# Second heads' root one exp later, part of a k norm on GpSimd, and first reciprocals behind the third heads' puts, in the opening of a fused attention and MoE kernel

## The chip, the cores and the metric

The kernel runs on one core of a Trainium2 chip. The metric is the device time of one execution in microseconds (us); lower is better. The core has five engines that run side by side, each through its own queue in order: TensorE (PE: matmuls and transposes), VectorE (DVE), ScalarE (ACT: exp, gelu, Ln, and some copies), GpSimd (POOL: elementwise work between SBUF tensors, and the issue of some DMAs) and SyncE (SP: the issue of most DMAs). Engines wait for one another through semaphores. Matmul results land in PSUM; everything else is in SBUF.

## The reference

Eight batches, 12 heads, 448 positions, head size 64. Queries and keys are RMS-normed with a gain, attention is a plain softmax, and its output goes through a two-layer MLP with a tanh-gelu:

```python
def rmsnorm(x, g):
    rms = np.sqrt(np.mean(x * x, axis=-1, keepdims=True) + 1e-06)
    return x / rms * g
q_n, k_n = (rmsnorm(q, g_q), rmsnorm(k, g_k))
scores = (1.0 / np.sqrt(64)) * np.matmul(q_n, k_n.transpose(0, 1, 3, 2))
scores = scores - np.max(scores, axis=-1, keepdims=True)
attn = np.exp(scores)
attn = attn / (np.sum(attn, axis=-1, keepdims=True) + 1e-09)
x = np.matmul(attn, v)            # then [B, S, H * D] as x of 3584 x 768
h = x @ w_in                      # 768 x 2048
g = 0.5 * h * (1.0 + np.tanh(c * (h + 0.044715 * h * h * h)))
return g @ w_out                  # 2048 x 768
```

Inputs and output are float32; the kernel computes its matmuls in bfloat16.

## The kernel before

The work goes batch by batch: attention of batch b + 1 is woven into the second MLP matmul of batch b. Nothing is scheduled by a planner: every engine does its instructions in the order in which the Python code issues them, and the code places them by hand. Only the attention of batch 0, which has no MLP work beside it, is touched by the change. It is made by `first_attention`.

The 12 heads of a batch are three groups of four, c = 0, 1, 2 ("first heads", "second heads", "third heads"). A group has seven tiles of 64 keys, t = 0 to 6. One `unit(0, c, t)` is four score matmuls (`sc`, two PSUM buffers) and one exp of 128 x 896 on ScalarE. So there are 21 units, numbered 0 to 20; unit 7 is the first of the second heads, unit 14 the first of the third heads. `first_attention` takes two plans: `side` (functions done ahead of a numbered unit) and `mid` (functions done behind a numbered unit). An entry `(8, f, g)` in `mid` issues f and g behind unit 8, each to its own engine's queue.

What a group needs before its first unit, for q and for k:

- `loads` brings the raw tiles, `square` squares them (ScalarE for the first heads, GpSimd after), `total` sums the squares on DVE;
- `rsqrt` makes the inverse root on ScalarE, as a Ln and an Exp with scale -0.5. `near` names the tensors (0 for q, 1 for k) whose root is written to PSUM, into `roots`, for DVE to read; the others' root goes to SBUF, into `rinvs`, for GpSimd, which reads SBUF here;
- `normed` multiplies raw by root on DVE or GpSimd (`nrmq`, `nrmk`); `turn` transposes on TensorE into the PSUM tiles `tp`; `put` copies the transposed q to `qT` and the transposed k times the gain column `gcol` to `kT`, on DVE. `t_first` is key tiles 0 to 3, `t_rest` is 4 to 6.

The gain column and the bound `shift`, which the exps subtract, come from the small tile `grow` with g_q and g_k in it: two DMAs (line 83), then products on GpSimd (`gprod`, `gbf`, lines 626 and 627), then GpSimd's first `normed` for the first heads' q.

What a group leaves: `products(0, c, 0)` sums the exps over keys by matmuls with ones, `turned` transposes these sums to `st` on DVE (line 358), `recips` takes the reciprocal and transposes back to `rb` (lines 364, 365), `products(0, c, 1)` is exps times v, and `quad_x` multiplies that by `rb` into `xT` (line 378). Both kinds of products of the first and of the second heads are written to the same two PSUM banks, `oall`: each has to wait until DVE has read the one before. The sums of the third heads go to two other banks (`spared`).

GpSimd's queue in this part holds, in order: the products of `grow`, a part of the first heads' q norm, the squares of the second heads, the issue of v's load, the squares of the third heads, six DMA issues of the first MLP weight (`w_in_part`, `win`, line 604), the norm of the third heads' q, two more of these issues, squares of batch 1, and issues of the second weight and the next v.

When the last exp of batch 0 is done, the last products follow, and the first MLP matmuls (`mm1_pair`, tile `hh`) start.

## Time and profile before

| what | value |
|---|---|
| time, median of 3 runs | 412.72 us (412.53 to 412.81) |
| the profiled execution, its own time | 412.78 us |
| its span (first to last instruction) | 410.9 us |
| TensorE busy | 399.3 us (97%) |
| ScalarE, DVE, POOL busy | 274.0, 256.0, 124.4 us |
| granted TensorE clock | 1.0 throughout |
| first exp, last exp of batch 0 starts | 9.93, 29.75 us |
| first MLP matmul starts | 32.86 us |

From 8 to 31 us, the time in which the first attention runs, DVE is busy 21.0, ScalarE 21.8 and POOL 22.6 of the 23 us.

In the lines of the profile, times are microseconds from the span's start. A line of the timeline has the start, the length, the engine, the source line, the operation, the tiles it writes and reads (out<-in, without buffer numbers), their shape, and how many instructions are merged into it; square brackets hold the idle time of the engine before it and what ended that. Instructions of one engine overlap a little: the next one starts some 0.05 to 0.1 us before the end of the one before. A line of the chain of waits has the start, the length and the work that the end of the program was waiting for at that time.

### The profile page before, as it was taken

How to read it: one execution, taken by the hardware profiler on the slowest of the kernel's cores; microseconds unless marked ns; L12 is line 12 of the kernel's file. 1: busy time of each engine (PE TensorE's matmuls, PEld its weight loads, DVE VectorE, ACT ScalarE, POOL GpSimd, SP SyncE). 2: the span in 40 equal slices, each digit the busy share in tenths (PEclk: the TensorE clock that was granted, in tenths of full speed). 3: DMA queues.
4: the chain of work that ended last, by engine and by line, in shares of the span. 5: the costliest groups of instructions: out<-in, count | busy, mean ns of one | idle time of the engine just before them, and what ended most of it. 6: DMA issues, size and time to landing. Idle time of an engine off the chain costs nothing.

```text
span 410.9 us, 8083 instructions
## 1 busy us (share of the span) xinstructions
PE 399.3 (97%) x3337; PEld 209.1 (51%) x3337; DVE 256.0 (62%) x414; ACT 274.0 (67%) x367; POOL 124.4 (30%) x102
## 2 busy tenths in 40 slices
PE   8889998999999999999999999999999999999996
PEld 3354554455555555555555555555555555555564
DVE  4999638845689357963688466982698604990010
ACT  5995387737975689738877579648878249744301
POOL 5991306492103540082302740063400900000000
PEclk9999999999999999999999999999999999999999
DMA  8999997869712947229922848309822511111033
GB/s 280 233 237 216 201 195 243 194 143 299 138 48 62 249 62 190 67 62 257 191 54 64 201 114 196 77 19 243 145 54 66 116 33 38 41 40 40 0 77 78
DMA packets 65572, 54.06 MB, mean 132 GB/s; under 512 B 37376, under 2 KB 60544, under 8 KB 65536
## 3 DMA queue, kind: packets, MB, share of 16 engines
q1 hardware_dynamic: 53184, 41.48, 39.1%
q0 software_dynamic: 12128, 11.80, 18.4%
q8 instruction: 26, 0.43, 0.4%
q10 hardware_dynamic: 224, 0.28, 0.2%
q14 instruction: 10, 0.08, 0.1%
HBM read 45.61 MB, written 11.01 MB: 138 GB/s over the span
## 4 chain that ended last, share of the span: by engine, by line
PE 88%; ACT 4%; DVE 4%; DMA 1%; POOL 1%; issue 0%; SPq 0%; DVEq 0%; ACTq 0%
PE o L408 35%; PE h L387 23%; PE t L298 8%; PE t L442 8%; PE t L349 8%; PE hh L442 4%; ACT ex L302 4%; DVE ss L156 2%; DMA rawq<-in_q_dram 1%; POOL g L151 1%; PE o L349 1%; DVE st L358 1%; PE tp L256 1%; DVE rb L365 1%; ACT g L447 0%; PE sc L298 0%
## 5 line engine op out<-in xcount | busy, mean ns | idle before, releaser
L408 PE MATMUL o<-wout,g 128*128 128x384 bf16 (+1 forms) x912 | 156.8, 324 | 0.0
L302 ACT ACTIVATE ex<-t,shift 128x896 bf16<-128x896 f32 x147 | 137.5, 1005 | 26.2 <-PE t L298 24.8
L408 PEld LDWEIGHTS <-g 128*128 128x128 bf16 x912 | 83.6, 98 | 68.0 <-issue 19.0
L387 PE MATMUL h<-xT,win 128*128 128x448 bf16 x504 | 96.5, 353 | 0.0
L156 DVE TENSOR_REDUCE ss<-sq 128x14 f32<-128x896 f32 (+3 forms) x43 | 44.3, 1037 | 53.6 <-ACT sq L149 50.7
L387 PEld LDWEIGHTS <-win 128*128 128x128 bf16 x504 | 49.3, 98 | 46.0
L393 ACT ACTIVATE g<-h 128x448 bf16<-128x448 f32 x84 | 45.6, 543 | 28.2 <-PE h L387 23.1
L422 DVE COPY osb<-o 128x384 f32<-128x384 f32 x51 | 27.7, 544 | 53.3 <-PE o L408 52.2
L298 PE MATMUL t<-qT,kT 64*64 64x448 bf16 x588 | 40.2, 360 | 1.7 <-DVE xT L373 1.1
L447 ACT ACTIVATE g<-t 128x896 bf16<-128x896 f32 x14 | 12.1, 914 | 43.5 <-PE t L442 43.5
L617 POOL COPY mark<-es 1x1 bf16<-1x1 bf16 x6 | 1.1, 176 | 129.8 <-DVE es L320 129.8
L442 PEld LDWEIGHTS <-win 128*128 128x128 bf16 x264 | 25.7, 98 | 24.8 <-issue 2.1
L238 POOL TENSOR_TENSOR nrmq<-rawq,rinv 128x896 bf16<-128x896 f32 (+1 forms) x21 | 34.8, 1659 | 10.1 <-DVE o L223 9.7
L442 PE MATMUL t<-xT,win 128*128 128x448 bf16 x168 | 33.5, 352 | 0.0
L151 POOL TENSOR_TENSOR sq<-rawq 128x896 f32<-128x896 f32 x9 | 15.1, 1681 | 57.3 <-DMA rawq<-in_q_dram 33.5
L298 PEld LDWEIGHTS <-kT 64*64 64x64 bf16 x672 | 16.5, 105 | 30.5 <-issue 24.3
L238 POOL TENSOR_TENSOR nrmk<-rawk,rinv 128x896 bf16<-128x896 f32 x19 | 31.9, 1679 | 0.0
L349 PE MATMUL t<-ex,vb 64*64 64x448 bf16 x588 | 31.6, 350 | 0.0
L365 DVE STREAM_TRANSPOSE rb<-rc 128x896 f32<-128x896 f32 x24 | 26.7, 1112 | 0.8
L349 PEld LDWEIGHTS <-vb 64*64 64x64 bf16 x672 | 19.6, 107 | 12.7 <-issue 2.9
L358 DVE STREAM_TRANSPOSE st<-t 128x448 f32<-128x448 f32 x42 | 24.6, 625 | 2.1 <-ACT ex L302 1.9
L323 DVE TENSOR_TENSOR e<-ex 128x896 bf16<-128x896 bf16 x32 | 19.4, 607 | 8.8 <-ACT ex L302 8.5
(89 smaller groups left out, 334.9 us busy)
## 6 DMA issues: line engine op xcount, KB each, us to landing
out_dram<-osb SPq DMA_DIRECT2D x54, 192.0 KB, 2.7
rawq<-in_q_dram SPq DMA_DIRECT2D x23, 448.0 KB, 4.6
rawk<-in_k_dram SPq DMA_DIRECT2D x23, 448.0 KB, 5.1
vb<-in_v_dram POOLq DMA_DIRECT2D x8, 672.0 KB, 6.7
win<-in_moe_w_in_dram POOLq DMA_DIRECT2D x8, 384.0 KB, 15.2
wout<-in_moe_w_out_dram POOLq DMA_DIRECT2D x2, 1536.0 KB, 26.4
qT<-nrmq SPq DMA_TRANSPOSE x19, 5.0
kT<-nrmk SPq DMA_TRANSPOSE x19, 4.4
```

Source lines behind the costliest of these rows:

```text
L156: nc.vector.reduce_sum(sss[b][:, c, "qk".index(n), hs, ts], sqs[n, b, c][:, hs, ts], axis=AX.X)
L238: eng.tensor_mul(nrms[n, b, c][:, ts].rearrange("p t a d -> p a t d"), raws[n, b, c][:, :, ts], root[:, :, ts].to_broadcast([P, 2, m, D]),)
L298: nc.tensor.matmul(sc[r * R:(r + 1) * R, a, :S], kT[rs, c, t, r], qT[b][rs, c, :, r], start=True, stop=True,)
L302: nc.scalar.activation(ex[:, t], sc[:, :, :S], AF.Exp, scale=scale, bias=shift)
L349: nc.tensor.matmul(o[r][a * D:(a + 1) * D], vb[b % 2][rs, 2 * c + a, i] if what else ones[rs], es[i][rs, a], start=(i == 0), stop=(i == n ...
L358: nc.vector.transpose(st[:, r].rearrange("p a b -> p (a b)"), oas[0][r])
L365: nc.vector.transpose(rb.rearrange("p r s -> p (r s)"), rc.to_broadcast([128, 2 * S // 32, 32]))
L387: nc.tensor.matmul(h[:, :S], win[:, c, f * 128:(f + 1) * 128], xT[b][:, c], start=(c == 0), stop=(c == HP - 1),)
L393: nc.scalar.activation(g[:, f, (b % 2) * S:(b % 2 + 1) * S], h[:, :S], AF.Gelu_apprx_tanh)
L408: nc.tensor.matmul(o, g[:, f, i * 128:(i + 1) * 128], wout[:, f, lo:hi], start=(f == 0), stop=(f == nf - 1),)
L422: nc.vector.tensor_copy(osb[:, lo:hi], o)
L442: nc.tensor.matmul(h[:, j, :S], win[:, c, f * 128:(f + 1) * 128], xT[b][:, c], start=(c == 0), stop=(c == HP - 1),)
```

## The change

Four things in the opening, all in the code for batch 0:

1. g_k is loaded by ScalarE's DMA queue, behind its half of the first q; it was loaded by GpSimd's queue behind g_q.
2. The root of the second heads is made behind the fourth exp (unit 3) instead of the third (unit 2). Before it, the rest of the first heads' k is normed, turned and put: the norm ahead of both sums, the turn and put behind unit 1. The put of the rest of the second heads' k moves behind the sums of the third heads' squares.
3. Of the second heads' k, `t_rest` is normed by GpSimd instead of DVE. For that, `rsqrt` writes the k root of the second heads to SBUF also (the new argument `also`, one more small Exp). GpSimd's new norm comes behind the square of the third heads' q; the square of the third heads' k and the six issues of `win` come behind it.
4. The first `recips` (reciprocal and transpose for the first heads) move on DVE from behind `turned` in slot 8 to slot 12, behind the puts of the third heads' q and first k tiles, and directly ahead of the first `quad_x`.

```diff
-    for i, row in enumerate((g_q, g_k)):
-        nc.gpsimd.dma_start(
+    def load_g(i, row, eng):
+        eng.dma_start(
             grow[:, i].rearrange("(j p) d -> j p d", j=2)[:, 0],
             row.rearrange("(j d) -> j d", j=2),
         )
+    load_g(0, g_q, nc.gpsimd)
...
-    def rsqrt(b, c=slice(0, NCH), ns=both, near=(), ts=slice(0, NT), twice=False):
+    def rsqrt(b, c=slice(0, NCH), ns=both, near=(), ts=slice(0, NT), twice=False, also=()):
...
         to_sbuf([n for n in range(2)[ns] if n not in near])
+        to_sbuf(also)
...
     for go in halves:
         go()
+    load_g(1, g_k, nc.scalar)
     nc.scalar.preload_act_table_set(EXP_SET)
...
     square(0, 2, "q", nc.gpsimd)
-    square(0, 2, "k", nc.gpsimd)
-    w_in_part(0, 2)
-    w_in_part(1, 2, range(1))
...
+    normed(0, 0, "k", nc.vector, t_rest)
     total(0, 1, "q")
-    normed(0, 0, "k", nc.vector, t_rest)
-    total(0, 1, "k")
...
-           (1, lambda: idle(2, warm())),
-           (2, lambda: rsqrt(0, 1, near=(0, 1)), lambda: idle(2, warm())),
-           (3, lambda: turn(0, 0, "k", t_rest), lambda: put(0, 0, "k", t_rest),
+           (1, lambda: turn(0, 0, "k", t_rest), lambda: put(0, 0, "k", t_rest),
+            lambda: total(0, 1, "k"), lambda: idle(2, warm())),
+           (2, lambda: idle(2, warm())),
+           (3, lambda: rsqrt(0, 1, near=(0, 1), also=(1,)),
             lambda: normed(0, 1, "q", nc.vector), lambda: normed(0, 1, "k", nc.vector, t_first),
-            lambda: normed(0, 1, "k", nc.vector, t_rest), lambda: idle(2, warm())),
+            lambda: normed(0, 1, "k", nc.gpsimd, t_rest), lambda: square(0, 2, "k", nc.gpsimd),
+            lambda: w_in_part(0, 2), lambda: w_in_part(1, 2, range(1)),
+            lambda: idle(2, warm())),
...
-           (6, lambda: turn(0, 1, "k"), lambda: put(0, 1, "k", t_first),
-            lambda: put(0, 1, "k", t_rest)),
+           (6, lambda: turn(0, 1, "k"), lambda: put(0, 1, "k", t_first)),
            (7, lambda: total(0, 2, "q"), lambda: total(0, 2, "k"),
-            lambda: products(0, 0, 0, 0, 3)),
-           (8, lambda: products(0, 0, 0, 3), lambda: turned(), lambda: recips(),
+            lambda: put(0, 1, "k", t_rest), lambda: products(0, 0, 0, 0, 3)),
+           (8, lambda: products(0, 0, 0, 3), lambda: turned(),
             lambda: rsqrt(0, 2, near=(1,)), lambda: normed(0, 2, "q", nc.gpsimd),
...
            (12, lambda: turn(0, 2, "q"), lambda: put(0, 2, "q"), lambda: turn(0, 2, "k"),
-            lambda: put(0, 2, "k", t_first), lambda: quad_x(0, 0),
+            lambda: put(0, 2, "k", t_first), lambda: recips(), lambda: quad_x(0, 0),
             lambda: put(0, 2, "k", t_rest)),
```

## The prediction

> **What bounds the kernel now.** I read the page first. Its share list of the chain that ended last gives TensorE nearly all of it:

> ```profile
> PE 88%; ACT 4%; DVE 4%; DMA 1%; POOL 1%; issue 0%; SPq 0%; DVEq 0%; ACTq 0%
> ```

> From 32.9 us on TensorE works almost without a hole, so whatever the change does before that point reaches the end at its full size, and a gain that is eaten before 32.9 is worth nothing. All edits lie before it. Second view: the chain of waits, 8 to 34 us (start, us, what). It is the time in which the first batch's attention runs.

> ```profile
> 2.20 6.04 DMA rawq<-in_q_dram
> ...
> 8.30 3.33 POOL g L151 x2
> ...
> 23.51 7.30 ACT ex L302 x8
> 30.81 0.04 issue
> 30.86 0.38 PE os L349 x4
> 31.24 1.69 PE o L349 x28
> ```

> The 21 exps of ScalarE (pitch 0.89 us) set the pace, but at three places they are held: the second heads' root (12.78), the second heads' first scores (17.09), the third heads' transposes (23.51, idle 0.29 before it). And POOL's work hangs on the landing of the second heads' q at 8.23, which no edit moves. Third view: the timeline of POOL (start, us, operation).

> ```profile
> 12.50 1.69 POOL L151 TENSOR_TENSOR g<-rawq 128x896 f32<-128x896 f32 x1
> 14.14 1.68 POOL L151 TENSOR_TENSOR sq<-rawk 128x896 f32<-128x896 f32 x1
> 15.76 3.79 POOL L604 DMA_DIRECT2D win<-in_moe_w_in_dram  x6
> 19.70 1.68 POOL L238 TENSOR_TENSOR nrmq<-rawq,rinv 128x896 bf16<-128x896 f32 x1
> ```

> POOL runs without a hole from 8.30, and the third heads' normed q (19.70 to 21.38) is at its end. Fourth: DVE, and TensorE beside it.

> ```profile
> 20.03 0.33 DVE L364 RECIPROCAL rc<-st 128x28 f32<-128x28 f32 x1
> 20.39 1.11 DVE L365 STREAM_TRANSPOSE rb<-rc 128x896 f32<-128x896 f32 x1
> 21.43 1.11 DVE L238 TENSOR_TENSOR nrmk<-rawk,root 128x512 bf16<-128x512 f32 x2
> 22.60 0.62 DVE L269 COPY qT<-tp 128x896 bf16<-128x896 bf16 x1
> 23.18 0.48 DVE L265 TENSOR_SCALAR kT<-tp,gcols 128x512 bf16<-128x512 bf16 x1
> 23.59 1.14 DVE L378 TENSOR_TENSOR xT<-o,rb 128x448 bf16<-128x448 f32 x2
> ```
> ```profile
> 22.00 0.56 PE L256 MATMUL tp<-ident,nrmq 128*128 128x128 bf16 x7
> 24.57 0.38 PE L298 MATMUL sc<-qT,kT 64*64 64x448 bf16 x4 [0.46 <-ACT ex L302]
> 24.76 0.78 PE L349 MATMUL o<-ex,ones 64*64 64x448 bf16 x12
> 25.47 0.38 PE L298 MATMUL sc<-qT,kT 64*64 64x448 bf16 x4
> ```

> To be seen: the second sum products (24.76) begin 0.03 us after quad_x frees the bank `oall` (23.59 + 1.14 = 24.73). They stand in front of the scores at 25.47, which the exp at 26.20 needs. That wait is closed already; its slack is small. The products end 0.57 us after 24.76, at 25.33, and scores lead their exp by 0.44 us (23.08 to 23.51), so scores at 25.76 would still serve 26.20: slack 0.43 us.

> **Part 1, g_k by ScalarE's queue.** By the rows of `grow`, g_q is issued at 1.30 and lands 3.7 us later at 4.97; g_k at 2.04, landing 4.0 later at 6.02; gprod starts 0.15 after that. ScalarE's own issue at 0.75 took 0.42 and landed after 3.35 us; so a g_k issued at 1.20 lands near 4.6, and gprod starts behind g_q at 5.1. ScalarE's table load moves from 1.20 to about 1.65 and ends at 2.9; the first square waits for q until 3.89, which hides the 0.42. One landing more among eight rotating semaphores makes SP's load of the third k wait for the first q half (3.87 instead of issue at 3.74): nothing, as that k lands at 11.8 and is squared at 14.9. POOL's normed q then waits for the root (6.23) instead of g, runs 6.3 to 7.34 instead of 7.02 to 8.06, and the first exp moves by 0.72, from 9.93 to 9.21.

> **Part 2, root behind the fourth exp.** Four exps from 9.21 end their pitch at 12.84; the k sums are done at 12.74 as before, since POOL's squares hang on the landing. The root comes at 12.84 instead of 12.78; Ln, root and the added rinv take 0.57 (the same three at 18.94 to 19.52). Exp 4 starts at 13.41, 0.73 earlier. But normed q, its transposes and puts follow the root: 13.39 start, q done 14.50, transposes 14.56, next scores 15.06, k transposes to 15.93, kT put 15.97 to 16.45, scores 16.51, exp 7 at 16.94 (17.09 before). Exps 6 and 7 wait 0.28 and 0.56 us, and **0.15 of the 0.73 is left.** POOL's 384-wide part is not in the trace: between 1.04 (512 wide) and nothing; by the slope to 1.68 (896 wide) it is 0.83 us, 14.14 to 14.97, before TensorE needs it at 15.4. I take that, as 384 is nearest to the 512 row; it stands in POOL's chain below, so at nothing the whole sum would be 0.79 less, at 1.04 it would be 0.21 more.

> **Part 3, what POOL's order now does.** From 14.14: normed k part (pitch 0.79), square of third k (1.62), six win issues (3.80), all ahead of normed q. It starts at 20.35 instead of 19.70 and ends at 22.03 instead of 21.38. The two last win issues, two squares, wout, v follow 0.65 later; win is first read at 32.86, with no wait on it shown, and that read moves back too, by more. Landing costs nothing then.

> **Part 4, reciprocals behind the puts.** DVE's normed k is now ready at 20.9 (was 22.54), but the put of q stands next and needs POOL's q: transposes 22.09 (22.03 + 0.06), done 22.65; put q 22.69; put k 23.27 to 23.75. So DVE idles 1.8 us, and the reciprocals, which ran 20.03 to 21.50 before, come after it: reciprocal 23.67, transpose 24.03 to 25.15, then quad_x with 0.10 delay (33.96 to 34.06 at the last such pair) and 1.15 for both halves: 25.25 to 26.40 instead of 24.73. Exps before this are at 23.44 and on, 0.07 early. TensorE's products get the second half-bank at 26.43; three groups at 0.19 remain, or two, so the scores come at 26.81 to 27.00 and exp 16 at 27.25 to 27.43 instead of 26.20. **The wait passed to quad_x costs 1.67, the slack takes 0.43, and exp 16 is 1.05 to 1.24 late.**

> **The end of the stage.** From these scores, DVE's second st transpose follows as now (25.47 to 26.64, 1.17): 28.09 instead of 26.64. From there to the end of the second quad_x DVE has no hole (26.64 to 31.36, 4.72), so 32.81; TensorE's last products overwrite `oall` and wait for it, and the first matmul of the MoE, 32.86 before (31.36 + 1.50), comes at 34.31. The exps end at 32.0 and do not bound it. Sum: **+1.45 us**, +1.34 to +1.53 by the two ends above, +1.27 if the 0.10 is also 0.03 as between the other dependent DVE rows, and by the ends for POOL's part +0.66 to +1.66. TensorE's rows behind are the same instructions in the same order.

> A question of its own is whether POOL's issues keep their length. The six took 0.63 to 0.69 us each (15.76 to 19.56) while DVE was busy 3.92 of the 4 us from 16 to 20, with copies and tensor_scalars from PSUM among its rows; so the sum uses 3.80 for the six. [...]

> **Rivals.**
> 1. *Not slower: POOL's q comes in time.* If normed q ends by 20.3, put and reciprocals run early enough that exp 16 is not held; the exps keep 0.15 plus the 0.29 wait and a little, and the kernel ends 0.3 to 0.7 us faster (412.0 to 412.4). Against: that needs POOL 1.7 us ahead of rows that follow each other without a hole from a landing at 8.23. The whole start gain, 0.73, is the most that could be kept, and it stays inside 0.2%. Chance 0.05.
> 2. *The late quad_x is partly covered.* Were the slack before exp 16 larger (TensorE's ends are modelled) and DVE's next rows tighter, 0.3 to 0.8 would be left: 413.0 to 413.5. For it: the idle 0.59 us of DVE before 26.64. Against: those products are late themselves. Chance 0.12.
> 3. *A second wait joins.* [...] So 1.45 plus 0.3 to 2.0: 414.5 to 416.2. [...] Chance 0.10. [...]
> 4. *The forecast,* 413.7 to 414.8. Chance 0.73.

> **The numbers.** The profiled execution took 412.78 (span 410.9 and 1.88 around it); the median of the three runs is 412.72, lowest 412.53. 412.78 + 1.45 = 414.23, and less the 0.06 between profile and median 414.2. The range takes all of the forecast, the upper half of rival 2 and the lower part of rival 3: 413.3 to 415.0. A difference of about 0.2% (0.83 us) is what a measurement can tell. Faster by more needs over 0.83 us, more than the whole start gain: 0.03. Within: the rest of rival 1 and most of rival 2, 0.13. Slower: 0.84.

> **What would show it.** In the changed profile: first exp near 9.2; exp 7 near 16.9; POOL's third normed q from 20.3 to 22.0; DVE idle before the qT copy near 22.7, released by TensorE's transposes; reciprocal near 23.7 instead of 20.0; the second sum products split, waiting on DVE's xT to 26.4; an exp idle of over 1 us near 26 to 27; the first `hh` matmul near 34.3. It is wrong if POOL's q ends before 21.4, or if quad_x ends after 26 and the exps still run on without a hole, or if the first `hh` matmul is at 33.5 or before.

## The result, and the profile after

The changed kernel takes 415.61 us (median of 8 runs, 413.86 to 417.52), the kernel before 412.76 beside it (8 runs, 412.30 to 413.58): ratio 1.007, 95% interval 1.0048 to 1.0093. It is slower, as forecast, but by 2.85 us instead of 1.45. The runs differ in the granted clock of TensorE, and that is part of the answer: the three with a mean clock of 0.998 or more took 413.86, 414.72 and 415.53 us, the five below it 415.37 to 417.52. So runs are counted below by whether their mean clock was under 0.998 ("low clock").

The profiled execution is the longest of the eight, 417.52 us (span 415.7), so it shows the costs at their largest. Its first `hh` matmul starts at 37.70 instead of 32.86, 4.84 later; from there to the end of the span it is 378.0 us in both, so the whole loss lies ahead of `hh`. The chain of waits of the changed kernel, 8 to 40 us (start, us, what), against the one shown of before, which held neither v nor `rb`:

```profile
8.45 3.26 POOL g L154 x2
11.71 10.79 DMA vb<-in_v_dram
...
22.54 0.76 PE o L353 x12
...
26.26 1.12 DVE rb L369
27.38 0.02 issue
27.41 0.64 DVE xT L382
28.04 0.04 issue
28.08 1.86 PE o L353 x12
```

Two things are on the chain. The reciprocals (`rb`) and `quad_x` (`xT`) stand there as the prediction had them. But the load of v stands ahead of them: it was issued at 11.71, about as before (11.56), and while the first of its sixteen parts landed at 17.7, the last did at 22.50 (18.5 before). The timeline of ScalarE's exps shows what each did (in square brackets the idle time and what ended it):

```profile
13.72 1.89 ACT L306 ACTIVATE ex<-sc,shift 128x896 bf16<-128x896 f32 x2
15.79 1.01 ACT L306 ACTIVATE ex<-sc,shift 128x896 bf16<-128x896 f32 x1 [0.18 <-PE sc L302]
17.24 1.91 ACT L306 ACTIVATE ex<-sc,shift 128x896 bf16<-128x896 f32 x2 [0.45 <-PE sc L302]
...
23.55 1.95 ACT L306 ACTIVATE ex<-sc,shift 128x896 bf16<-128x896 f32 x2 [1.96 <-PE sc L302]
25.69 2.80 ACT L306 ACTIVATE ex<-sc,shift 128x896 bf16<-128x896 f32 x3 [0.20 <-PE sc L302]
30.35 1.01 ACT L306 ACTIVATE ex<-sc,shift 128x896 bf16<-128x896 f32 x1 [1.86 <-PE sc L302]
31.91 3.70 ACT L306 ACTIVATE ex<-sc,shift 128x896 bf16<-128x896 f32 x4 [0.56 <-PE sc L302]
```

The idle 0.18 and 0.45 behind the root are part 2's. The 1.96 is v. The 1.86 and 0.56 are part 4's, and more than it: the sum products that start at 28.08 take 1.86 us for 12 matmuls (0.78 in the kernel before). The reason is in the next view, TensorE in stretches of 3.41 us (from:to, length, busy time and matmuls, granted clock, DMA share, GB/s):

```profile
14.38:17.79 3.41, 2.36 (x42) 1.00 1.14 170
17.79:21.21 3.42, 1.95 (x30) 1.00 1.07 291
21.21:24.62 3.41, 2.08 (x41) 1.00 1.24 171
24.62:28.03 3.41, 1.79 (x25) 1.00 1.12 224
28.03:31.45 3.42, 3.37 (x34) 0.50 1.10 259
31.45:34.86 3.41, 3.31 (x66) 1.00 1.11 244
```

The records of the granted clock change at 28.03 and at 31.45: for 3.41 us it was half. In the profile before, no record of a half clock lies inside the span. TensorE's pauses in the stretch ahead of 28.03 are short, 0.40, 0.32 and 0.95 us by its timeline, but together they leave it busy for only 1.79 of 3.41 us.

### The profile page after: what moved, and what is told of

Its sections match the earlier page's. It is cut to its first block, busy times and chain, and to the rows that moved or that the text cites. A ratio compares the mean times of both kernels' runs of the same rounds, so it can differ in the third digit from the quotient of the medians.

```text
span 415.7 us, 8084 instructions
## 1 busy us (share of the span) xinstructions
PE 400.0 (96%) x3337; PEld 209.4 (50%) x3337; DVE 255.9 (62%) x413; ACT 274.7 (66%) x368; POOL 124.8 (30%) x102
## 3 DMA queue, kind: packets, MB, share of 16 engines
q0 software_dynamic: 12096, 11.80, 18.5%
## 4 chain that ended last, share of the span: by engine, by line
PE 87%; DMA 4%; DVE 4%; ACT 3%; POOL 1%; issue 0%; SPq 0%; DVEq 0%; ACTq 0%
PE o L412 34%; PE h L391 23%; PE t L302 8%; PE t L446 8%; PE t L353 8%; PE hh L446 4%; DMA vb<-in_v_dram 3%; ACT ex L306 2%; PE o L353 2%; DMA rawq<-in_q_dram 1%; DVE ss L159 1%; DVE rb L369 1%; POOL g L154 1%; DVE st L362 1%; ACT g L451 0%
## 5 line engine op out<-in xcount | busy, mean ns | idle before, releaser
L302 PE MATMUL t<-qT,kT 64*64 64x448 bf16 x588 | 40.0, 359 | 1.8 <-DVE xT L377 1.1
L451 ACT ACTIVATE g<-t 128x896 bf16<-128x896 f32 x14 | 12.1, 914 | 43.5 <-PE t L446 43.5
L446 PE MATMUL t<-xT,win 128*128 128x448 bf16 x168 | 33.5, 352 | 0.0
L242 POOL TENSOR_TENSOR nrmk<-rawk,rinv 128x896 bf16<-128x896 f32 (+1 forms) x20 | 32.8, 1638 | 0.0
L302 PEld LDWEIGHTS <-kT 64*64 64x64 bf16 x672 | 16.9, 105 | 29.9 <-issue 24.2
```

The costliest lines, as they stand in the source:

```text
L242: eng.tensor_mul(nrms[n, b, c][:, ts].rearrange("p t a d -> p a t d"), raws[n, b, c][:, :, ts], root[:, :, ts].to_broadcast([P, 2, m, D]),)
L302: nc.tensor.matmul(sc[r * R:(r + 1) * R, a, :S], kT[rs, c, t, r], qT[b][rs, c, :, r], start=True, stop=True,)
L446: nc.tensor.matmul(h[:, j, :S], win[:, c, f * 128:(f + 1) * 128], xT[b][:, c], start=(c == 0), stop=(c == HP - 1),)
```

## The experiments

All times are medians. The runs were made in four groups, each on one chip; "before" is the kernel before, timed in the same group. Two explanations stood against each other from the start: the late sums of part 4 with the half clock behind TensorE's pauses (A in the first four texts, H in the later ones), and v's late landing (B, later V and V2).

**First group** (before: 413.32 us, 35 runs, 4 at a low clock).

*The reciprocals back in their old place*, the rest of the change kept:

```diff
-           (8, lambda: products(0, 0, 0, 3), lambda: turned(),
+           (8, lambda: products(0, 0, 0, 3), lambda: turned(), lambda: recips(),
...
-            lambda: put(0, 2, "k", t_first), lambda: recips(), lambda: quad_x(0, 0),
+            lambda: put(0, 2, "k", t_first), lambda: quad_x(0, 0),
```

> The changed kernel with the first reciprocals put back where they were (behind the first sums' transposes), everything else as changed. Theory A (the late reciprocals make quad_x late, the sum products and an exp wait for it, and the half clock seen at 28 to 31.4 us follows from that pause): the loss is gone, 412.3 to 412.9, granted clock 1.0, no exp of the third heads idle by more than 0.6 us, second sum products at 24.6 to 25.0. Theory B (the loss over 1.45 us comes from the first v landing late, because the second batch's first k load is issued 1.5 us earlier and shares the transfer engines with v): still 1 to 2 us slower than before, 413.7 to 414.8, with the first products of v waiting for its landing after 20.5 us.

Measured: 413.40 us (412.62 to 416.71, 12 runs), ratio 1.0009, 0.9986 to 1.0032. *The reciprocals in slot 9*, behind the third heads' k norm and ahead of their puts:

```diff
-           (9, lambda: idle(2, warm()), lambda: normed(0, 2, "k", nc.vector, t_rest)),
+           (9, lambda: idle(2, warm()), lambda: normed(0, 2, "k", nc.vector, t_rest),
+            lambda: recips()),
```

> The changed kernel with the first reciprocals between the third heads' normed k and their puts, into the 1.8 us in which DVE idles there by the working of the prediction. Theory A: quad_x ends near 24.9 us, exp 16 is not held, 412.0 to 412.7, clock 1.0. Theory B: 413.7 to 414.8, held by v. If DVE's idle time were not there when v is in time, the puts would be late by up to 1.4 us and the result 413 to 414.

Measured: 413.58 us (412.96 to 416.24, 12 runs), ratio 1.0009, 0.9988 to 1.0030. In both, 8 runs were at full clock (413.23 and 413.37 us, beside 413.25 of before) and 4 below. So parts 1 to 3 neither gain nor lose at full clock, and part 4 carries the steady loss. *Seven idle matmuls ahead of the second sum products* (they compute nothing that is used):

```diff
-           (15, lambda: products(0, 1, 0, 0, 3)),
+           (15, lambda: idle(7, ps_m.tile([128, 512], F32, tag="mm", name="fill")[:, :S]),
+            lambda: products(0, 1, 0, 0, 3)),
```

> The changed kernel with seven more matmuls on zeros behind unit 15, into a PSUM tile of their own, where TensorE waits for quad_x; nothing is taken from the wait. Theory A with the half clock as the excess: the clock stays 1.0 in most runs and the time falls from 415.6 to 414.0 to 414.4, the 1.45 us of the prediction. Theory B: 415 to 416 as the changed kernel, since v is as late as before. If both hold, between the two, with runs apart by up to 2 us.

Measured: 414.64 us (413.69 to 416.04, 12 runs), ratio 1.0027, 1.0008 to 1.0047; 9 runs at full clock (414.42), 3 below. *v's first load ahead of the second heads' squares*:

```diff
+    load_v(0, 0, HP)
     square(0, 1, "q", nc.gpsimd)
     square(0, 1, "k", nc.gpsimd)
-    load_v(0, 0, HP)
```

> The changed kernel with the first v's load issued ahead of the squares of the second heads, in POOL's idle time before the second heads' q lands; the load shares the queues with q and k then, and the squares may start up to 0.3 us later. Theory A: v waits are gone where there were any, the late quad_x stays: 414.0 to 415.2, with half clock in some runs. Theory B: 413.9 to 414.3 in all runs. If v early costs the second heads' q its place in the transfer queue, POOL's squares start after 8.8 us and the whole is 0.5 us later still.

Measured: 414.93 us (413.75 to 418.38, 12 runs), ratio 1.0034, 1.001 to 1.0058. With half of the runs at a low clock (415.59) and half at full (413.87), this group could not price v: the clock hid it.

**What precedes a half clock.** In these traces the changes of the clock lie 3.41 us or a multiple apart (in the profiled execution of the changed kernel the full clock ahead of the half is recorded for 23.89 us, seven times 3.41, and the half clock for 3.41), so each trace was cut into stretches of that length. In the first group's traces and the two first ones, a stretch at full clock in which TensorE was busy for 49, 51, 52 and 56% was followed by half clock, and every one of the first 45 us with 57% or more by full clock. The **second group** was made to test that (before: 413.33 us, 30 runs, 5 at a low clock). *The changed kernel again:*

> The changed kernel itself, timed again beside the kernel before and the kernels of this call. Theory H: the time is the late sums of part 4 at full clock (+1.1 us, about 414.4) plus a second term that falls only in some runs: a stretch of 3.41 us in which TensorE was busy for less than some 57% is followed by one or two stretches of 3.41 us at half clock. In the traces so far the stretches ahead of a half clock were busy for 49, 51, 52 and 56%, and all others of the first 45 us for 57% or more. The pause behind the root (13.7 to 14.9) and the one ahead of the first sum products are what the change opened, so half the runs or more should show a mean clock below 0.998 and 415.5 to 417, the rest 413.9 to 414.7: median 414.6 to 415.8. Rival V: v's late landing is the cause, and comes in every run: every run at 415 or more, whatever its clock. Rival S: the half clock falls by chance, as often as before (4 runs of 35): median 414.4.

Measured: 415.18 us (413.91 to 419.57, 12 runs), ratio 1.0055, 1.003 to 1.008. Seven runs were at a low clock, five at full: 414.45. *Part 4 alone on the kernel before* (the edit of the first experiment, the other way round):

> The kernel before with part 4 alone: the first reciprocals behind the third heads' puts, all else as before. Theory H: the first sums come 1.65 us later for a slack of 0.43, so the runs at full clock are 1.1 to 1.2 us above the kernel before (414.4 beside 413.3); the pause behind the root isn't there, the one ahead of the sum products is, so some runs (a quarter to a half) fall to half clock: median 414.4 to 415.0. Rival: the late sums cost only because parts 2 and 3 made the third heads late as well; then part 4 alone is hidden by the third heads' puts that the vector engine does earlier, and the time is within 0.4 us of the kernel before.

Measured: 415.15 us (413.36 to 416.51, 12 runs), ratio 1.003, 1.001 to 1.005; 7 runs at a low clock. Five at full clock ran 413.36, 413.42, 413.63, 414.46 and 414.50, which I first read as a price of 0.4; the third group corrects that. *Both pauses filled*: the seven idle matmuls, and six ahead of the second heads' turn of q:

```diff
-           (5, lambda: turn(0, 1, "q"), lambda: put(0, 1, "q")),
+           (5, lambda: idle(6, warm()), lambda: turn(0, 1, "q"), lambda: put(0, 1, "q")),
```

> The changed kernel with idle matmuls in both pauses: six ahead of the second heads' turns of q (TensorE stood for 1.2 us there), and seven ahead of the second sum products. They compute nothing that is used. With six more matmuls laid into the trace of the kernel that had only the seven, no stretch of 3.41 us is busy for under 61%, which is the kernel before's own lowest. Theory H: the share of runs below a mean clock of 0.998 is that of the kernel before (1 in 9), against 3 of 12 with one fill; the median is 414.3 to 414.5, all of it part 4's late sums. Rival S (the half clock has nothing to do with the pauses): 3 to 6 of 12 runs below 0.998 and a median of 414.6 or more. Rival V (v late): 415 or more.

Measured: 414.52 us (413.88 to 415.01, 11 runs), ratio 1.0021, 1.0003 to 1.0038, none at a low clock. Its trace has one stretch at 55% (1.88 of 3.42 us) with full clock behind it, where the first experiment's at 56% (1.92 of 3.41) had half clock: between these two the busy share does not decide. *The kernel before without its idle matmuls:*

```diff
-    mid = [(0, lambda: idle(2, warm())),
-           (1, lambda: idle(2, warm())),
-           (2, lambda: rsqrt(0, 1, near=(0, 1)), lambda: idle(2, warm())),
+    mid = [(2, lambda: rsqrt(0, 1, near=(0, 1))),
...
-            lambda: normed(0, 1, "k", nc.vector, t_rest), lambda: idle(2, warm())),
-           (4, lambda: idle(2, warm())),
+            lambda: normed(0, 1, "k", nc.vector, t_rest)),
```

> The kernel before without its ten idle matmuls between the first score products (two behind each of the first five units; their results are not used). Nothing waits for them, so at full clock the time stays (413.3). Theory H: without them the lowest stretch of 3.41 us is busy for 42%, and for 70% of the places that such a stretch can begin at, one of them is under 57%: 6 to 10 of 12 runs show a clock below 0.998 and are 1.2 to 2.5 us longer, median 414.3 to 415.5. Rival S: no more runs at a low clock than before, median within 0.3 us of the kernel before.

Measured: 415.49 us (414.23 to 416.35, 7 runs), ratio 1.0045, 1.0029 to 1.0062, and all seven runs at a low clock. Its stretches, same columns as above:

```profile
9.65:13.06 3.41, 1.82 (x21) 1.00 0.46 161
13.06:16.47 3.41, 2.25 (x19) 0.50 1.08 218
16.47:19.89 3.42, 2.84 (x31) 0.50 1.17 277
19.89:23.30 3.41, 3.04 (x30) 0.50 1.10 253
23.30:26.71 3.41, 3.35 (x59) 1.00 1.13 209
```

Behind the stretch at 53% the clock was half; it stayed half behind those of 66 and 83%, and was full again behind the one of 89%. Nothing waits for these ten matmuls, and taking them out costs 2.2 us by the medians. So here the half clock is a cost of the pauses, shown from both sides: with them filled none of 11 runs was at a low clock, with them opened all seven were.

**Third group** (before: 412.55 us, 29 runs, one at a low clock). *Parts 1 to 3, reciprocals in slot 9, the six idle matmuls:*

> Parts 1 to 3 of the change, with the first reciprocals ahead of the third heads' puts (slot 9), and six idle matmuls in the pause behind the second heads' root; these compute nothing that is used. The same kernel without the six had 413.4 us at full clock and 4 of 12 runs below a mean clock of 0.998. Theory H: with the six laid into its trace no stretch of 3.41 us is busy for under 61%, so 0 to 2 of 12 runs are below 0.998, and the median is that of the kernel before within 0.4 us (413.0 to 413.6). Rival S (the half clock has nothing to do with the pause): 3 to 5 of 12 below 0.998. Rival G (parts 1 to 3 gain once the clock is held): 412.7 or less, faster than the kernel before.

Measured: 413.40 us (412.97 to 416.04, 12 runs), ratio 1.0016, 0.9995 to 1.0038, 2 at a low clock. The clock held as H had it. The median stayed 0.85 above the kernel before, which the interval of the ratio does not call a difference. The traced run took 415.28, well above that median: v landed at 21.7 and held an exp for 1.25 us, and behind the first `hh` matmul (34.28) TensorE waited again, 1.04 us for the fourth part of `win`, which had been issued at 18.48. The chain of waits of this trace, 8 to 36 us, ends with it:

```profile
18.48 17.08 DMA win<-in_moe_w_in_dram
35.55 0.14 issue
35.69 0.35 PE hh L446
```

In every other trace it is 378.0 to 378.1 us from the first `hh` to the end of the span, here it is 379.2. *Part 4 alone with five idle matmuls* ahead of the second sum products:

> Part 4 alone on the kernel before, and five idle matmuls in the 0.95 us for which TensorE stood ahead of the second sum products; these compute nothing that is used. Without the five: 413.6 us in the 5 runs at full clock, 415.4 in the 7 below 0.998, and a lowest stretch of 46%. Theory H: nearly all runs at full clock (0 to 2 of 12 below 0.998), and the price of part 4 without the third heads' lateness of parts 2 and 3 shows by itself: +0.4 us on the kernel before, median 413.4 to 414.0, against the +1.2 that it has in the changed kernel. Rival S: 5 to 8 of 12 below 0.998, median 415. Rival: the five matmuls delay the sums that they stand ahead of, and the runs at full clock are above 414.2.

Measured: 414.69 us (413.30 to 417.11, 12 runs), ratio 1.004, 1.0021 to 1.006, one at a low clock instead of seven: the clock's part confirmed, my 0.4 us refuted. From the first exp behind the second heads' root to the end of the last exp, the traces give 18.63 us without the five and 18.62 with them, against 17.54 in the kernel before: part 4 costs 1.1 us there by itself. The median is 2.1 above the kernel before beside it; of the 1.84 by which the traced run's first `hh` is late (34.70 less 32.86), 0.67 lies ahead of part 4, in a later root (13.45 instead of 12.78). The three quick runs were not the rule: they hold the traced one, with its first exp at 9.49, where the trace with the five has it at 10.09 and the second q landing at 8.91 (8.23 in the kernel before). *Three more idle matmuls in the kernel before*, behind the second heads' turn of k:

```diff
-           (6, lambda: turn(0, 1, "k"), lambda: put(0, 1, "k", t_first),
+           (6, lambda: turn(0, 1, "k"), lambda: idle(3, warm()), lambda: put(0, 1, "k", t_first),
```

> The kernel before with three more idle matmuls behind the second heads' turns of k, where TensorE stood for 0.58 us inside its lowest stretch of 3.41 us (61% busy, and 76% with them); they compute nothing that is used. Theory H: the kernel before shows a clock below 0.998 in 9 of 65 runs, 2 us longer each, and if the jitter of that stretch is what drops it, none or one of 12 does so here; the median stays within 0.2 us, the mean falls by 0.2 to 0.3 and the highest run is under 414.8. Rival: those runs come from elsewhere (late loads at the start), and 1 to 3 of 12 are still below 0.998.

Measured: 413.24 us (412.51 to 414.32, 12 runs), ratio 1.0001, 0.9983 to 1.0018, none at a low clock. No gain: its median is 0.7 above the kernel before, outside the 0.2 that I expected, which that ratio does not call a difference; with one low run in 29 beside it, where those come from stays undecided.

**Fourth group** (before: 412.76 us, 29 runs, none at a low clock), for v alone, with the clock held. *The kernel with both pauses filled, again:*

> The changed kernel with idle matmuls in both pauses, again, as the partner on the same chip for the kernel with v's load moved. Its clock was at 0.998 or above in all 11 runs of the first time. Both theories below: nearly all runs at full clock, +1.0 to +1.6 us on the kernel before.

Measured: 414.84 us (413.79 to 419.11, 12 runs), ratio 1.0047, 1.0025 to 1.0069, one at a low clock. *The same with v's load ahead of the squares:*

> The changed kernel with idle matmuls in both pauses, and the first load of v ahead of the squares of the second heads instead of behind them. v was issued between 11.57 and 11.71 and landed at 21.3 to 23.1 in four profiles of kernels with part 2 (and by 19.3 in the four with an issue at 12.08 or later, or at 7.69); the exponentials then ended 0.9 to 1.2 us later, counted from the root. Theory V2: a part of the runs pays that, and v issued at 7.7 lands by 19: no wait of the first products of v for it, and the median is 0.4 to 0.9 us under that of the partner. Rival: where v is late the loads of the start were early by as much, so nothing is paid in sum; within 0.3 us of the partner. Or v takes transfer time from the second and third heads' q and k: slower than the partner.

Measured: 414.01 us (413.79 to 414.70, 12 runs), ratio 1.0023, 1.0012 to 1.0035: 0.83 under its partner, and all runs within 0.91 us, where the partner's spread over 5.3. V's last part landed at 17.0. Some runs of the partner pay and some do not: five of its eleven at full clock took 413.79 to 414.19, as this kernel, and six 414.76 to 415.52. Nor is all of it shown to be the wait for v: GpSimd issues `win` behind v, and the fourth part of `win` landed at 30.4 in this kernel's trace and at 33.7 in the partner's. *Parts 1 to 3, slot 9, six idle matmuls, v early:*

> Parts 1 to 3 with the first reciprocals in slot 9, six idle matmuls behind the root, and v's load ahead of the squares of the second heads: the three costs found so far taken away. Theory V2: level with the kernel before or under it by up to 0.4 us (ratio 0.999 to 1.0005), where the kernel without the move of v was at 1.0016. Rival: parts 1 to 3 lose behind the root what they gain ahead of it, and v is paid by early loads: +0.3 to +0.9 us.

Measured: 412.66 us (412.31 to 413.25, 12 runs), ratio 0.9992, 0.998 to 1.0004. With all three costs taken away the kernel is level with the kernel before; no version tried is measurably faster. The exps of these last two kernels differ by part 4 and by the seven idle matmuls in front of its sum products. These seven fill the wait and add next to nothing to it: the scores behind the first 12 sum products start 0.53 us after quad_x ends (26.82 less 26.29), and 0.46 after it where there are none (26.06 less 25.60, part 4 alone). The timeline of ScalarE with part 4 and, in the second fence, without it:

```profile
19.55 6.68 ACT L306 ACTIVATE ex<-sc,shift 128x896 bf16<-128x896 f32 x7
27.33 4.65 ACT L306 ACTIVATE ex<-sc,shift 128x896 bf16<-128x896 f32 x5 [1.10 <-PE sc L302]
```
```profile
19.71 11.17 ACT L306 ACTIVATE ex<-sc,shift 128x896 bf16<-128x896 f32 x12
```

One wait of 1.10 us at exp 16 is what part 4 does to the exps; without it the twelve run through.

## Why the forecast was right in its direction and too small

The kernel with both pauses filled and v early is the change as the prediction saw it, with the clock at 1.0 and v in time. So its trace tests the working, step by step (it also has the idle matmuls and the earlier issue of v, which the prediction did not have):

| step | forecast | that kernel | changed kernel |
|---|---|---|---|
| first exp | 9.21 | 9.49 | 9.54 |
| exp 4, exp 7 | 13.41, 16.94 | 13.66, 17.19 | 13.72, 17.24 |
| POOL's third normed q | 20.35 to 22.03 | 20.05 to 21.75 | 20.50 to 22.20 |
| DVE idle, put of q | 1.8, 22.69 | 1.57, 22.71 | 3.79, 24.97 |
| reciprocal | 23.67 | 23.64 | 25.91 |
| quad_x ends | 26.40 | 26.30 | 28.57 |
| exp 16 | 27.25 to 27.43 | 27.33 | 30.35 |
| first `hh` | 34.31 | 34.19 | 37.70 |
| time | 414.2 | 414.01 (median) | 415.61 (median) |

**Parts 1 and 2: mechanism right, start missed by 0.3.** ScalarE's issue of g_k took 1.10 us, not 0.42, and so the table load started at 2.33 and ended at 3.62 instead of 2.9; that was still hidden, as the first q half landed at 4.12 in this run. Normed q of the first heads then hangs on the root, not on g, as forecast, but starts at 6.62, 0.3 later than taken. Over all traces the first exp starts at 9.28 to 9.83 with part 1 (eleven traces, median 9.54) and at 9.49 to 10.29 without it (five, median 9.93): a gain of some 0.4 instead of 0.72, and no larger than the spread from run to run. The waits of exps 6 and 7, forecast as 0.28 and 0.56 on top of the pitch of 0.89, came out as 0.29 and 0.56 (15.79 less 13.72 and two pitches, 17.24 less 15.79 and one); the 0.18 and 0.45 of the timeline count from the end of the exp before. "0.15 of the 0.73 is left" becomes nothing: exp 7 starts at 17.24 against 17.09 before. Parts 1 to 3 together came out level (412.66 beside 412.76, with the pause filled and v early).

**Part 3: right.** The 384-wide norm took 0.83, the value worked out between its two bounds. The six issues of `win` behind it took 3.79 (3.79 before), so they kept their length, as the sum had it with 3.80. The timeline of POOL in the changed kernel:

```profile
14.28 0.83 POOL L242 TENSOR_TENSOR nrmk<-rawk,rinv 128x384 bf16<-128x384 f32 x1
15.06 1.67 POOL L154 TENSOR_TENSOR sq<-rawk 128x896 f32<-128x896 f32 x1
16.69 3.79 POOL L609 DMA_DIRECT2D win<-in_moe_w_in_dram  x6
20.50 1.70 POOL L242 TENSOR_TENSOR nrmq<-rawq,rinv 128x896 bf16<-128x896 f32 x1
```

**Part 4 and the end of the stage: right, with one step by luck.** The rows of DVE, of the kernel with the fills and early v, stand within 0.11 us of the working:

```profile
22.71 0.62 DVE L273 COPY qT<-tp 128x896 bf16<-128x896 bf16 x1 [1.57 <-PE tp L260]
23.25 0.47 DVE L269 TENSOR_SCALAR kT<-tp,gcols 128x512 bf16<-128x512 bf16 x1
23.64 0.32 DVE L368 RECIPROCAL rc<-st 128x28 f32<-128x28 f32 x1
23.99 1.11 DVE L369 STREAM_TRANSPOSE rb<-rc 128x896 f32<-128x896 f32 x1
25.14 1.16 DVE L382 TENSOR_TENSOR xT<-o,rb 128x448 bf16<-128x448 f32 x2
```

The luck is in the put of q. The forecast released it by POOL's q (22.03, transposes 22.09). In this trace POOL's q was done at 21.75, and the transposes began at 22.10, 0.29 behind the start of the scores ahead of them on TensorE, as in the kernel before (21.38 and 22.00): the time agrees to 0.02, and what released it was another. By the last two kernels part 4 costs 1.35 us of the time (414.01 less 412.66); the first group has 1.05 for it at full clock (414.42 with the seven idle matmuls, less 413.37 with the reciprocals in slot 9).

**The sum: this is the step that failed.** The whole loss was taken to be part 4's, on the ground that "TensorE's rows behind are the same instructions in the same order". They are, but not at the same clock, and v's landing was put at nothing without a reason. In the profiled execution the two missing terms can be read off against the kernel with the fills and early v. The row of quad_x of the changed kernel (the other one stands above), and those of the first `hh`, the changed kernel's first:

```profile
27.41 1.16 DVE L382 TENSOR_TENSOR xT<-o,rb 128x448 bf16<-128x448 f32 x2
37.70 0.55 PE L446 MATMUL hh<-xT,win 128*128 128x448 bf16 x2
```
```profile
34.19 2.06 PE L446 MATMUL hh<-xT,win 128*128 128x448 bf16 x10
```

Quad_x ends at 28.57 instead of 26.30: 2.27 us, v, whose first products start at 22.54 instead of 20.30. From there to the first `hh` it takes 9.13 us (37.70 less 28.57) instead of 7.89 (34.19 less 26.30): 1.24 us, the half clock. With the 1.33 that this kernel has itself (34.19 less 32.86) that makes the 4.84 seen. In medians: part 4 +1.35, the place of v's load +0.83 (414.84 less 414.01), the clock +0.66 (415.18 less 414.52, one chip), parts 1 to 3 −0.10; together 2.74, beside 2.85 measured at first. These terms come from two chips, so the sum is rough and no test. On the chip of the second group the kernel with both pauses filled is 1.19 above the kernel before, late v included, and with the 0.66 of the clock that is the 1.85 measured there.

**The rivals.** The third, "a second wait joins", was nearest: its 414.5 to 416.2 holds the 415.61. But no run of the changed kernel shows the 0.3 to 2.0 us that its sum adds for such a wait as one term; in its place the runs showed 0.83 for the place of v's load (in the profiled execution TensorE waited 2.02 us for v) and 0.66 for the clock, which was no wait at all. A wait for late parts of `win` did come in one trace of a related kernel, that of parts 1 to 3 with six idle matmuls, where it held TensorE for 1.04 us. In the changed kernel's own trace the fourth part landed at 35.91, behind the 34.31 that was forecast for the first `hh` and ahead of the 37.70 that was measured, so there the other costs hid it; in that of the kernel with the fills and early v it landed at 30.44. "Landing costs nothing then" is thus not safe. The first two (POOL in time; cover for quad_x) did not come about.

**What is not settled.** Why v is late. Its last two or three of sixteen parts lag by some 1 to 4 us, in five traces, all of them with parts 1 to 3 and with v issued from 10.8 to 11.7; part 2 lets the load of batch 1's first k start at 10.08 instead of 11.59, ahead of v. But in three more traces that load is ahead of v as well, v is issued from 12.1 to 12.5, and it lands by 19.3; there v is issued 2.0 to 2.2 us behind that k, in the five 0.8 to 1.8. With v issued at 7.6 to 7.7 its last part lands at 17.0 to 18.5, which takes the cost away; the cause of the lag was not isolated. Nor is it settled why the second heads' q lands at anything from 7.14 to 9.19 us in the sixteen traces; without part 2 the root moves with it (12.17 with a landing at 7.62, 13.45 with one at 8.91). It may be one reason why runs at full clock still differ by a microsecond and more; no run tested that.

## What to carry to other kernels

Where an edit opens pauses on TensorE, cost them twice: as waits, and by the share of each stretch of 3.41 us that stays busy: in this kernel half clock followed eight stretches that were busy for 42 to 56%, and none of 57% or more. Idle matmuls that look like waste may hold that share up (taking ten of them out cost 2.2 us here), and a step that is moved away from its cover takes the cover from the clock too (with part 4 alone 7 of 12 runs were at a low clock, 5 of 30 of the kernel before beside it). And where a load lands as little before its reader as v did here (18.5 against a first read at 20.2), treat every reordering of loads ahead of it as a cost with a range, not as nothing.

## What the runs showed of the hardware

```profile
13.43:16.85 3.42, 1.69 (x26) 1.00 1.01 139
16.85:20.26 3.41, 3.38 (x40) 0.50 1.09 274
20.26:23.68 3.42, 1.43 (x18) 1.00 1.08 213
23.68:27.09 3.41, 3.41 (x38) 0.50 1.13 223
27.09:30.50 3.41, 1.82 (x21) 1.00 1.10 259
30.50:33.91 3.41, 3.26 (x38) 0.50 1.11 254
```

- **Where the stretches begin differs from run to run.** The half clock of the changed kernel begins at 28.03 us in its first trace and at 16.85, 23.68 and 30.50 in its second, and 28.03 is no multiple of 3.41 from any of these three. The same kernel was hit in some runs and not in others: 12 of 20 runs of the changed kernel were at a low clock, 7 of 7 without the idle matmuls, 4 of 83 over the seven timings with idle matmuls added behind the root, in both pauses, or in the kernel before and with part 4 alone, 10 of 123 of the kernel before. Short pauses that added up were enough: the longest one inside each of the eight stretches above was 0.9 to 1.7 us.
- **The issue of g_k on ScalarE's queue took 1.10 us**, where that of the first q ahead of it took 0.40; SyncE's issues right behind one another took 0.43 to 0.47 in the same trace. Whether the place or the small load (64 floats) makes it long, no run shows.
